# An adaLN block with a spectral filter and a gated bilinear MLP, forward and backward: the backward norms formed from two independent halves, the gate folded into a transform table, first activations of the tail loaded in the loop

## Chip, cores and metric

The kernel runs on one core of a Trainium2 chip. The metric is the device time of one execution in microseconds (us). The core's engines are named as in the profile: PE (TensorE matmul; PEld is its weight load), DVE (VectorE), ACT (ScalarE), POOL (GpSimd) and SP (SyncE, which here issues most of the DMA transfers). Each engine works through its own instructions in order and waits on semaphores.

## What is computed

The reference computes a block with two residual branches and the gradients of all its inputs (reference.py, cut):

```python
mod = (_silu(c) @ w_mod).reshape(c.shape[0], 6, 1, -1)
sa, ca, ga, sb, cb, gb = ...
h = _layernorm(x, axis=-1) * (1 + ca) + sa
x = x + ga * _A_ref(h, A_w_r, A_w_i)      # y = irfft2(rfft2(h) * (w_r + 1j * w_i))
h = _layernorm(x, axis=-1) * (1 + cb) + sb
x = x + gb * _B_ref(h, ...)               # ((h @ w_gate) * (h @ w_up)) @ w_down
...
_out, _vjp = jax.vjp(_f, A_x, A_w_r, A_w_i, B_w_gate, B_w_up, B_w_down, c, w_mod)
_grads = _vjp(grad_out)
```

The sequence has S = 2048 rows (16 tiles of 128), D = 576 channels, F = 4608 hidden channels; inputs and outputs are bf16. The gradient through a layer norm with normalised input n, reciprocal deviation r, and incoming gradient g (already times 1 + c) is r * (g - mean(g) - n * mean(g * n)). Here it is added to the gradient that comes along the residual path.

## The kernel before

**The whole.** The kernel first does the forward of the spectral branch with matrices in place of the FFT (about the first 210 us), then one loop over 36 blocks of 128 hidden channels, then a tail. The loop (`for fb in range(NFB)`) forms gate and up products (gup, L647), their gradients, the weight gradients of gate, up and down (u57p, L594) and the gradient of the MLP's input (u8p, L676), which DVE adds up over all blocks in SBUF (acc, L681). A block takes 28 us. For u8p the transposed weights of four blocks at a time lie in a tile wT, in a pool of two buffers (`wtp`); the last of them, for blocks 32 to 35, leaves the other buffer without further use. The gradient of the MLP's hidden product, ghh, is loaded per block on POOL's queue; the transposing DMAs of hh, gg and gu are on SP's.

**The tail** starts when tile t of acc is whole; its instructions are interleaved with the last block's by a scheduler that works with priorities (`HEAD_START`, `SPREAD`), so the order in the queues is not the order in the text. The PE instructions of the last blocks' u57p, and of out_0's matrix product (u3p, L1127), serve as fill between the steps of the tail. The tail has these stages:

- T1 (L852 to L921), 16 tiles in a pipeline of four steps. `t1_norm`: from acc(t) it forms ghr (ACT copy, L869), gn = acc * (1 + cb) with its row sum (DVE, L872), the row sum of gn * n2 (jk, L874), the two means as a pair ab (L876), then u = gn * r + ab0 (ACT, L878), v = n2 * ab1 + u (DVE, L880), gxr = v + goc (DVE, L881; goc is a tile of grad_out, and gxr is stored as gx1_d for T3) and gyr = gxr * ga (DVE, L883; ga_h is the gate as a row, copied to all partitions). `t1_turn`: five PE transposes of gyr (trp, L888), an ACT copy (gyT, L890), and the column sums and diagonals csA, csB, csC (L784, L791) for the modulation's gradients, which use ghr, gxr, n2 and y (tile yc). `t1_cols`: gyT times the row transform's table RD (zp, L908), copied by ACT (zt, L909). `t1_rows`: zt times the table G1 (vp, L915 and L916), copied into Vp.
- T2 (L963 to L1011), 19 chunks: the filter in the frequency domain, with transposes trv (L971) and try_ (L995), products xp and apt, and wn, the weights w_r and w_i (one load of all of it, L930 on).
- T3 (L1024 to L1069), 16 tiles in a pipeline of three steps: the inverse transform (upa, upb, yp) and `t3_norm`, the backward of the first norm, with the same chain as T1: gn (L1049), jk (L1051), abt (L1053), u (L1055, ACT), v (L1057), ob = v + gxc (L1059), stored as the gradient of x.
- the rest of u3p with its outputs, and the gradients of the modulation's weight (`section`, L812).

**Loads of the tail.** SP loads, for each pair of tiles of T1, n2c, goc and yc (288 KB each, L857), with the tables RD (730 KB) behind the first pair and G1 (1536 KB) behind the second (an explicit order, `behind(ld["order"])`). All three tiles have two buffers. The w_down weights for u3p are loaded in two tiles, wdA (15 blocks) and wdB (21 blocks), beside tiles hl of hh (L1102, L1113), issued after a T1 load (`after`) and as soon as their place in SBUF is free. SBUF space is given by pools, and a new tile waits for the last user of the addresses it takes.

Of the kernel before, what the change touches and what calls it, by code (L numbers as in the profile page):

```python
# [9 lines left out]
FP32 = mybir.dt.float32  # L10
# [9 lines left out]
NT = 16  # L20
# [64 lines left out]
def build(ctx, tc, A_x, A_w_r, A_w_i, B_w_gate, B_w_up, B_w_down, c_in, w_mod, grad_out,  # L85
# [36 lines left out]
    dsl_col = glob.tile([128, 5], FP32, name="dsl_col")  # L122
    ident = glob.tile([128, 128], BF, name="ident")
# [419 lines left out]
    with ExitStack() as ms:  # L543
# [8 lines left out]
        ga_h = c1a.tile([128, D], BF, name="ga_h")  # L552
# [4 lines left out]
        with ExitStack() as bs:  # L557
# [18 lines left out]
            nc.sync.dma_start(ga_h[:], modb_d[:, MGA, :])  # L576
# [42 lines left out]
            def wT_load(f0, after):  # L619
                nb = min(FBT, NFB - f0)  # L620
                wT = wtp.tile([128, 2, FBT, D], BF, name="wT")
# [67 lines left out]
            for fb in range(NFB):  # L689
# [7 lines left out]
                if fb == 0:  # L697
                    wTs[0] = wT_load(0, turns[-1:] * 5)
                ghh = ghp.tile([128, NT, 128], BF, name="ghh")
# [31 lines left out]
    with ExitStack() as ts:  # L731
# [108 lines left out]
        with ExitStack() as r1:  # L840
# [5 lines left out]
            rings = {k: c1b.tile([128, 3, DP], BF, name=k) for k in ("gyr", "ghr", "gxr")}  # L846
# [3 lines left out]
            ld, gyTs, zts = {"order": []}, {}, {}  # L850

            def t1_norm(t):  # L852
                if t % 2 == 0:
                    for k, src in (("n2c", n2_d), ("goc", go_v), ("yc", y_d)):
                        ld[k] = c1.tile([128, 2, D], BF, name=k)
                        with behind(ld["order"]):
                            ins = nc.sync.dma_start(ld[k][:], src[:, t:t + 2, :])  # L857
                        if t == 4:
                            ld["after"] = ins.ins
                    if t < 4:  # L860
                        ld["order"] = [ins.ins]
                        with behind(ld["order"]):
                            for k, tag in ((("RD", "tA"),), (("G1", "tB"), ("BD2", None), ("BDA", None)))[t // 2]:
                                T[k] = load_table(tl0, k, tag)
                        ld["order"] = [tab_ins[k]]
                    ld[t // 2] = (ld["n2c"], ld["yc"])
                n2 = ld["n2c"][:, t % 2, :]
                gh, gx, gy = (rings[k][:, t % 3, 0:D] for k in ("ghr", "gxr", "gyr"))
# [5 lines left out]
                nc.vector.scalar_tensor_tensor(out=jk[:], in0=gn[:], scalar=1.0, in1=n2, op0=MUL, op1=MUL, accum_out=s12[:, 1:2])  # L874
# [10 lines left out]
            def t1_turn(t):  # L885
                pt = ps_fp.tile([128, 5, 128], BF, name="trp", tag="fp")
                for m in range(5):
                    nc.tensor.transpose(pt[:, m, :], rings["gyr"][:, t % 3, wide(m)], ident[:])  # L888
# [338 lines left out]
```

## Time and profile before

Three executions took 1585.04, 1588.66 and 1589.61 us; the profile is of another execution of 1585.66 us.

| what | value |
|---|---|
| time, median of 3 runs | 1588.66 us |
| profiled execution, its time | 1585.66 us |
| profiled execution, its span | 1583.9 us |
| mean granted PE clock | 0.99 |
| PE busy | 1526.4 us, 96% of the span |
| DVE busy | 1043.3 us, 66% |
| ACT busy | 559.4 us, 35% |
| POOL busy | 172.3 us, 11% |
| DMA traffic | 280.33 MB, mean 177 GB/s |

How to read it: the profile shows one execution. "Busy" is the time in which an engine executes instructions; a line of a group gives the source line, the engine and operation, output and inputs by the program's names, partitions x elements, then busy time and mean ns of one, then the idle time ahead of such instructions and what ended it. A line of waits gives engine, operation and line, then what released it, the total in us, how often, and the longest. In a table by stretch, each engine's busy time is followed by its number of instructions in brackets; PEclk is the granted clock of PE as a share of the full one, and DMA share the busy share of the 16 DMA engines. Matmuls are pipelined, so the mean duration of one (286 ns for a 288-column one) is longer than the distance between two; 32 u57p in a row took 3.92 us.

### The profile page before, as it was taken

How to read it: one execution, taken by the hardware profiler on the slowest of the kernel's cores; microseconds unless marked ns; L12 is line 12 of the kernel's file. 1: busy time of each engine (PE TensorE's matmuls, PEld its weight loads, DVE VectorE, ACT ScalarE, POOL GpSimd, SP SyncE). 2: the span in 40 equal slices, each digit the busy share in tenths (PEclk: the TensorE clock that was granted, in tenths of full speed). 3: DMA queues.
4: the chain of work that ended last, by engine and by line, in shares of the span. 5: the costliest groups of instructions: out<-in, count | busy, mean ns of one | idle time of the engine just before them, and what ended most of it. 6: DMA issues, size and time to landing. Idle time of an engine off the chain costs nothing.

```text
span 1583.9 us, 29938 instructions
## 1 busy us (share of the span) xinstructions
PE 1526.4 (96%) x11300; PEld 1028.1 (65%) x11306; DVE 1043.3 (66%) x2626; ACT 559.4 (35%) x1120; POOL 172.3 (11%) x285
## 2 busy tenths in 40 slices
PE   6999999999999999999999999999999979799997
PEld 4665543566666666667666666766666666577775
DVE  6866663766666666666666666666666765678655
ACT  6667732322222222222222222222222356465022
POOL 0001221110010101001010100101000002000232
PEclk9999999999999999999999999999999999999999
DMA  9879997868685795877767786858976777547775
GB/s 323 268 197 235 289 261 211 172 133 158 123 177 114 159 153 118 168 132 155 141 148 136 143 163 122 173 116 144 139 141 137 193 207 200 212 144 214 278 228 156
DMA packets 485252, 280.33 MB, mean 177 GB/s; under 512 B 407634, under 2 KB 452435, under 8 KB 484211
## 3 DMA queue, kind: packets, MB, share of 16 engines
q1 hardware_dynamic: 459922, 185.50, 54.9%
q0 software_dynamic: 25184, 92.92, 19.7%
q8 instruction: 88, 1.44, 0.4%
q14 instruction: 58, 0.47, 0.1%
HBM read 108.48 MB, written 82.31 MB: 120 GB/s over the span
## 4 chain that ended last, share of the span: by engine, by line
PE 81%; DVE 6%; DMA 5%; issue 4%; ACT 3%; POOL 0%; SPq 0%; ACTq 0%; DVEq 0%; POOLq 0%
PE u57p L594 26%; PE u8p L676 18%; PE gup L647 16%; PE u4p L408 7%; PE u3p L1127 4%; PE gup L642 2%; DMA Xn<-xn_d 2%; DMA n2c<-n_d 2%; PE yp L186 1%; PE zp L908 1%; ACT u L1055 1%; PE zp L346 1%; DVE ln_st L151 1%; DMA xc<-in_A_x_dram 1%; DMA hh_sf<-hhT 1%
## 5 line engine op out<-in xcount | busy, mean ns | idle before, releaser
L681 DVE TENSOR_TENSOR acc<-acc,u8p 128x288 f32<-128x288 f32 x1088 | 489.2, 454 | 314.6 <-PE u8p L676 314.2
L676 PE MATMUL u8p<-wT,ggT 128*128 128x288 bf16 x1152 | 327.5, 286 | 1.7 <-DVE acc L681 1.7
L676 PE MATMUL u8p<-wT,guT 128*128 128x288 bf16 x1152 | 327.2, 286 | 0.0
L647 PE MATMUL gup<-h2T,wgu 128*128 128x512 bf16 x1152 | 294.9, 379 | 0.0
L597 ACT CAST so<-u57p 128x288 bf16<-128x288 f32 x216 | 86.0, 398 | 521.4 <-PE u57p L594 515.5
L594 PE MATMUL u57p<-gon,hh_sf 128*128 128x288 bf16 x1152 | 188.5, 286 | 0.5 <-DMA hh_sf<-hhT 0.5
L594 PE MATMUL u57p<-h2p,gg_sf 128*128 128x288 bf16 x1152 | 187.9, 286 | 0.0
L594 PE MATMUL u57p<-h2p,gu_sf 128*128 128x288 bf16 x1152 | 185.9, 286 | 0.0
L647 PEld LDWEIGHTS <-wgu 128*128 128x128 bf16 x1152 | 109.5, 98 | 98.8 <-issue 17.1
L676 PEld LDWEIGHTS <-ggT 128*128 128x128 bf16 x1152 | 112.6, 98 | 67.2 <-issue 14.0
L408 PE MATMUL u4p<-goT,wdT 128*128 128x512 bf16 x656 | 151.6, 380 | 0.6 <-DVE goT L380 0.5
L676 PEld LDWEIGHTS <-guT 128*128 128x128 bf16 x1152 | 112.7, 98 | 55.8 <-issue 2.2
L1127 PEld LDWEIGHTS <-hl 128*128 128x128 bf16 x1152 | 111.9, 99 | 32.9 <-issue 5.9
L594 PEld LDWEIGHTS <-hh_sf 128*128 128x128 bf16 x1152 | 112.7, 98 | 29.2 <-DMA hh_sf<-hhT 0.8
L594 PEld LDWEIGHTS <-gu_sf 128*128 128x128 bf16 x1152 | 112.5, 98 | 28.4
L594 PEld LDWEIGHTS <-gg_sf 128*128 128x128 bf16 x1152 | 112.5, 98 | 28.2
L649 ACT CAST gT<-gup 128x512 bf16<-128x512 f32 x144 | 84.3, 586 | 130.7 <-PE gup L647 130.7
L649 ACT CAST uT<-gup 128x512 bf16<-128x512 f32 x144 | 84.3, 585 | 73.5 <-PE gup L647 73.5
L408 PEld LDWEIGHTS <-wdT 128*128 128x128 bf16 x656 | 61.4, 98 | 73.1 <-issue 8.0
L1127 PE MATMUL u3p<-wdB,hl 128*128 128x288 bf16 x672 | 94.8, 290 | 5.3 <-DMA wdB<-in_B_w_down_dram 5.3
L660 POOL DMA_DIRECT2D hhT_d<-hhT x36 | 33.2, 921 | 504.4 <-DVE hhT L651 475.5
L141 ACT CAST ghh_st<-u4p 128x512 bf16<-128x512 f32 x88 | 51.2, 585 | 65.2 <-PE u4p L408 63.7
(357 smaller groups left out, 1701.7 us busy)
## 6 DMA issues: line engine op xcount, KB each, us to landing
ghhT_d<-ghh_st POOLq DMA_DIRECT2D x36, 512.0 KB, 4.4
ghh<-ghhT_d POOLq DMA_DIRECT2D x36, 512.0 KB, 7.3
hhT_d<-hhT POOLq DMA_DIRECT2D x36, 512.0 KB, 6.6
hl<-hhT_d SPq DMA_DIRECT2D x32, 576.0 KB, 7.2
out_dram<-woT SPq DMA_DIRECT2D x72, 128.0 KB, 2.0
wdn<-in_B_w_down_dram SPq DMA_DIRECT2D x18, 288.0 KB, 3.9
out_dram<-so SPq DMA_DIRECT2D x36, 144.0 KB, 2.6
wgu<-in_B_w_gate_dram SPq DMA_DIRECT2D x18, 256.0 KB, 3.4
```

The lines of the kernel that those rows point to most:

```text
L141: nc.scalar.copy(dst, src)
L151: nc.vector.bn_stats(out=st[:, t, h, :], in_=xt[:, t, h * 288:(h + 1) * 288])
L408: nc.tensor.matmul(pt[:], lhsT=wdTs[k][:, j, m, :], rhs=goT[:, 4 * sb4:4 * sb4 + 4, m, :], start=(m == 0 and n == 5), stop=(m == n - 1))
L594: mm = nc.tensor.matmul(pw[0][:, 0:288], lhsT=sf[:, t, :], rhs=rhs_n[:, t, h * 288:(h + 1) * 288], start=(t == 0), stop=(t == NT - 1))
L597: nc.scalar.copy(so[:, h * 288:(h + 1) * 288], pw[0][:, 0:288])
L642: nc.tensor.matmul(pts[-1][:], lhsT=wgu[r, 8, jw * 128:(jw + 1) * 128], rhs=h2T[r, 4 * sb4:4 * sb4 + 4, 4, :], start=True, stop=False)
L647: nc.tensor.matmul(pts[k][:], lhsT=wgu[:, 4 * wi_ + m, jw * 128:(jw + 1) * 128], rhs=h2T[:, ts_, m, :], start=False, stop=(m == 3))
L649: nc.scalar.copy((gT, uT)[wi_][:, ts_, :], pts[k][:])
L660: nc.gpsimd.dma_start(hhT_d[:, :, fb, :].rearrange("tp f x -> f tp x"), hhT[:].rearrange("f (tp ti) p -> f tp (ti p)", ti=2))
L676: nc.tensor.matmul(pu[:, 0:288], lhsT=l_, rhs=r_, start=(k == 0), stop=(k == len(mms) - 1))
L681: nc.vector.tensor_tensor(out=dst, in0=dst, in1=pu[:, 0:288], op=ADD)
L1127: mm = nc.tensor.matmul(p2[:, 0:288], lhsT=hls[fb // 9][:, fb % 9, ti * 128:(ti + 1) * 128], rhs=(wdA[:, fb] if fb < 15 else wdB[:, fb - 1 ...
```

## The change

Three things are done.

1. In both backward norms the result is formed from two halves. w = gn * r + (residual gradient) needs neither mean and is formed by DVE right behind the sums; u = n * ab1 + ab0 is formed by ACT from n instead of from gn; a last addition w + u gives gx (T1) or ob (T3). In T1 and in T3 this last part is a step of its own in the pipeline (`t1_gx`, `t3_out`), one turn later than the sums. The instruction v is gone.
2. The gate ga no longer multiplies the rows. gyr and its ring are gone, the transposes take gxr, and the rows of the table RD are multiplied by ga instead, once, by five ACT instructions on 128 x 584 elements in block NFB-2 of the loop. For this, ga is loaded as a column (two small DMAs, a POOL memset, a DVE copy), and the row ga_h is gone.
3. RD and the first two tiles of n2 are loaded by POOL in block NFB-3 of the loop, into a tile `early` in the pool of wT. n2 of tiles 2 to 7 is loaded in three pieces to one tile n2a at the head of the tail, in the place (tag tA) where RD was; n2c serves tiles 8 to 15 alone, and its first two loads are issued at t = 2 and 4. G1 is loaded at t = 0; goc has three buffers. The explicit order among these loads is gone.

The number of PE instructions is the same. In the built program, the loads of wdA stand behind opca_h on SP and wait for PE instructions of T1, and no u3p stands before T2's second apt.

```diff
--- before.py
+++ after.py
@@ -120,6 +120,8 @@
     rstd1g = glob.tile([128, NT], FP32, name="rstd1g")
     rstd2g = glob.tile([128, NT], FP32, name="rstd2g")
     dsl_col = glob.tile([128, 5], FP32, name="dsl_col")
+    ga_bf = glob.tile([128, 5], BF, name="ga_bf")
+    ga_col = glob.tile([128, 5], FP32, name="ga_col")
     ident = glob.tile([128, 128], BF, name="ident")
     make_identity(nc, ident[:])
     ones_f = glob.tile([128, 128], FP32, name="ones_f")
@@ -549,7 +551,7 @@
         c1acm = tc.tile_pool(name="c1a", bufs=1, side="right", reuse_waits="tile")
         c1a = c1acm.__enter__()
         opcb_h = c1a.tile([128, D], BF, name="opcb_h")
-        ga_h = c1a.tile([128, D], BF, name="ga_h")
+        ahead = {}
 
         def acc(t):
             return acc1[:, t, :] if t < 9 else acc2[:, t - 9, :]
@@ -573,7 +575,11 @@
             u8ps = bpool("u8ps", 3, PSUM)
             u57ps = bpool("u57ps", 2, PSUM)
             nc.sync.dma_start(opcb_h[:], modb_d[:, MCB, :])
-            nc.sync.dma_start(ga_h[:], modb_d[:, MGA, :])
+            nc.gpsimd.memset(ga_bf[:], 0.0)
+            with nc.allow_non_contiguous_dma(reason="tiny column load"):
+                nc.sync.dma_start(ga_bf[:, 0:4], modb_d[0, MGA, 0:512].rearrange("(m q) -> q m", q=128))
+                nc.sync.dma_start(ga_bf[0:64, 4:5], modb_d[0, MGA, 512:576].rearrange("(m q) -> q m", q=64))
+            nc.vector.tensor_copy(ga_col[:], ga_bf[:])
             pend = []
             NSO = 4
             so4 = sop.tile([128, NSO, DP], BF, name="so4")
@@ -618,7 +624,7 @@
 
             def wT_load(f0, after):
                 nb = min(FBT, NFB - f0)
-                wT = wtp.tile([128, 2, FBT, D], BF, name="wT")
+                wT = wtp.tile([128, 2, FBT, D], BF, name="wT", tag="wT")
                 for wi_, wsrc in enumerate((B_w_gate, B_w_up)):
                     for m in range(5):
                         K = KD[m]
@@ -696,6 +702,16 @@
                             eng.dma_start(wgu[64 * wi_:64 * wi_ + 64, 8, :], wsrc[512:576, fb * 128:(fb + FBW) * 128])
                 if fb == 0:
                     wTs[0] = wT_load(0, turns[-1:] * 5)
+                if fb == NFB - 3:
+                    early = wtp.tile([128, 2, FBT, D], BF, name="early", tag="wT")[:].rearrange("q i j d -> q (i j d)")
+                    RDg = early[:, 0:10 * FP].rearrange("q (m c f) -> q m c f", m=5, c=2)
+                    nc.gpsimd.dma_start(early[:, 0:10 * FP], tab_d["RD"][:, :])
+                    for t in range(2):
+                        ahead[t] = early[:, 10 * FP + t * D:10 * FP + t * D + D]
+                        nc.gpsimd.dma_start(ahead[t], n2_d[:, t, :])
+                if fb == NFB - 2:
+                    for m in range(5):
+                        nc.scalar.activation(out=RDg[:, m], in_=RDg[:, m], func=ACT.Copy, scale=ga_col[:, m:m + 1])
                 ghh = ghp.tile([128, NT, 128], BF, name="ghh")
                 with later(1, fb):
                     nc.gpsimd.dma_start(ghh[:].rearrange("f t p -> f (t p)"), ghhT_d[fb * 128:(fb + 1) * 128, :])
@@ -843,58 +859,75 @@
             csA = ps_cs.tile([128, 512], FP32, name="csA")
             csB = ps_cs.tile([128, 512], FP32, name="csB")
             csC = ps_cs.tile([128, 512], FP32, name="csC")
-            rings = {k: c1b.tile([128, 3, DP], BF, name=k) for k in ("gyr", "ghr", "gxr")}
+            rings = {k: c1b.tile([128, 3, DP], BF, name=k) for k in ("ghr", "gxr")}
             with tc.high_priority(HEAD_START):
                 for k in rings:
                     nc.vector.memset(rings[k][:, :, D:DP], 0.0)
-            ld, gyTs, zts = {"order": []}, {}, {}
+            ld, gyTs, zts = {}, {}, {}
+
+            def t1_loads(t):
+                if t == 0:
+                    n2a = tl0.tile([128, 6, D], BF, name="n2a", tag="tA")
+                    for k in range(3):
+                        ld["n2a"] = nc.sync.dma_start(n2a[:, 2 * k:2 * k + 2, :], n2_d[:, 2 + 2 * k:4 + 2 * k, :])
+                        for i in range(2):
+                            ahead[2 + 2 * k + i] = n2a[:, 2 * k + i, :]
+                        if k == 0:
+                            ld[0] = [c1.tile([128, 2, D], BF, name=n_, bufs=b_) for n_, b_ in (("goc", 3), ("yc", 2))]
+                            for tl_, src in zip(ld[0], (go_v, y_d)):
+                                nc.sync.dma_start(tl_[:], src[:, 0:2, :])
+                            T["G1"] = load_table(tl0, "G1", "tB")
+                    for k in ("BD2", "BDA"):
+                        T[k] = load_table(tl0, k)
+                if t % 2 == 0 and t:
+                    ld[t // 2] = [c1.tile([128, 2, D], BF, name=n_, bufs=b_) for n_, b_ in (("goc", 3), ("yc", 2))]
+                    for tl_, src in zip(ld[t // 2], (go_v, y_d)):
+                        ins = nc.sync.dma_start(tl_[:], src[:, t:t + 2, :])
+                    if t == 4:
+                        ld["after"] = ins.ins
+                if t in (2, 4, 12, 14):
+                    t_ = t + 6 if t < 8 else t
+                    n2c = c1.tile([128, 2, D], BF, name="n2c")
+                    nc.sync.dma_start(n2c[:], n2_d[:, t_:t_ + 2, :])
+                    for i in range(2):
+                        ahead[t_ + i] = n2c[:, i, :]
 
             def t1_norm(t):
-                if t % 2 == 0:
-                    for k, src in (("n2c", n2_d), ("goc", go_v), ("yc", y_d)):
-                        ld[k] = c1.tile([128, 2, D], BF, name=k)
-                        with behind(ld["order"]):
-                            ins = nc.sync.dma_start(ld[k][:], src[:, t:t + 2, :])
-                        if t == 4:
-                            ld["after"] = ins.ins
-                    if t < 4:
-                        ld["order"] = [ins.ins]
-                        with behind(ld["order"]):
-                            for k, tag in ((("RD", "tA"),), (("G1", "tB"), ("BD2", None), ("BDA", None)))[t // 2]:
-                                T[k] = load_table(tl0, k, tag)
-                        ld["order"] = [tab_ins[k]]
-                    ld[t // 2] = (ld["n2c"], ld["yc"])
-                n2 = ld["n2c"][:, t % 2, :]
-                gh, gx, gy = (rings[k][:, t % 3, 0:D] for k in ("ghr", "gxr", "gyr"))
+                t1_loads(t)
+                gh = rings["ghr"][:, t % 3, 0:D]
                 nc.scalar.copy(gh, acc(t))
                 s12 = c1.tile([128, 2], FP32, name="s12")
                 gn = c1.tile([128, D], BF, name="gn2")
                 nc.vector.scalar_tensor_tensor(out=gn[:], in0=acc(t), scalar=1.0, in1=opcb_h[:], op0=MUL, op1=MUL, accum_out=s12[:, 0:1])
                 jk = c1.tile([128, D], BF, name="jk2", bufs=1)
-                nc.vector.scalar_tensor_tensor(out=jk[:], in0=gn[:], scalar=1.0, in1=n2, op0=MUL, op1=MUL, accum_out=s12[:, 1:2])
+                nc.vector.scalar_tensor_tensor(out=jk[:], in0=gn[:], scalar=1.0, in1=ahead[t], op0=MUL, op1=MUL, accum_out=s12[:, 1:2])
                 ab = c1.tile([128, 2], FP32, name="ab2")
                 nc.vector.tensor_scalar(out=ab[:], in0=s12[:], scalar1=-1.0 / D, scalar2=rstd2g[:, t:t + 1], op0=MUL, op1=MUL)
+                w = c1.tile([128, D], BF, name="w2")
+                nc.vector.scalar_tensor_tensor(out=w[:], in0=gn[:], scalar=rstd2g[:, t:t + 1], in1=ld[t // 2][0][:, t % 2, :], op0=MUL, op1=ADD)
+                ld["ab", t], ld["w", t] = ab, w
+
+            def t1_gx(t):
+                gx = rings["gxr"][:, t % 3, 0:D]
                 u = c1.tile([128, D], BF, name="u2")
-                nc.scalar.activation(out=u[:], in_=gn[:], func=ACT.Identity, bias=ab[:, 0:1], scale=rstd2g[:, t:t + 1])
-                v = c1.tile([128, D], BF, name="v2", bufs=1)
-                nc.vector.scalar_tensor_tensor(out=v[:], in0=n2, scalar=ab[:, 1:2], in1=u[:], op0=MUL, op1=ADD)
-                nc.vector.tensor_tensor(out=gx, in0=v[:], in1=ld["goc"][:, t % 2, :], op=ADD)
+                ab = ld["ab", t]
+                nc.scalar.activation(out=u[:], in_=ahead[t], func=ACT.Identity, bias=ab[:, 0:1], scale=ab[:, 1:2])
+                nc.vector.tensor_tensor(out=gx, in0=ld["w", t][:], in1=u[:], op=ADD)
                 nc.gpsimd.dma_start(gx1_d[:, t, :], gx)
-                nc.vector.tensor_tensor(out=gy, in0=gx, in1=ga_h[:], op=MUL)
 
             def t1_turn(t):
                 pt = ps_fp.tile([128, 5, 128], BF, name="trp", tag="fp")
                 for m in range(5):
-                    nc.tensor.transpose(pt[:, m, :], rings["gyr"][:, t % 3, wide(m)], ident[:])
+                    nc.tensor.transpose(pt[:, m, :], rings["gxr"][:, t % 3, wide(m)], ident[:])
...
-                n2c, yc = ld[t // 2]
+                yc = ld[t // 2][1]
                 if t == 0:
                     add_zero(csA, csB, csC, first=True)
...
-                diag(csA, csB, 288, gh, n2c[:, t % 2, :])
+                diag(csA, csB, 288, gh, ahead[t])
                 diag(csC, csB, 352, gx, yc[:, t % 2, :])
                 if t == NT - 1:
                     add_zero(csA, csB, csC, first=False)
@@ -905,7 +938,7 @@
                     zp = ps_fp.tile([128, 512], FP32, name="zp", tag="fp")
                     for m in range(5):
                         with behind(fill[t - 1:t] if t else []):
-                            nc.tensor.matmul(zp[:, :FP], lhsT=gyTs[t][:, m, :], rhs=T["RD"][:, m, cc, :], start=(m == 0), stop=(m == 4))
+                            nc.tensor.matmul(zp[:, :FP], lhsT=gyTs[t][:, m, :], rhs=RDg[:, m, cc, :], start=(m == 0), stop=(m == 4))
                     nc.scalar.copy(zt[:, cc, :], zp[:, :FP])
 
             def t1_rows(t):
@@ -916,7 +949,7 @@
...
 
-            steps = [t1_norm, t1_turn, t1_cols, t1_rows]
+            steps = [t1_norm, t1_gx, t1_turn, t1_cols, t1_rows]
             for k in range(NT + len(steps) - 1):
                 with tc.high_priority(HEAD_START + SPREAD * k):
                     for s_ in reversed(range(len(steps))):
@@ -1051,13 +1084,9 @@
             nc.vector.scalar_tensor_tensor(out=jk[:], in0=gn[:], scalar=1.0, in1=n1, op0=MUL, op1=MUL, accum_out=s12[:, 1:2])
             ab = c3.tile([128, 2], FP32, name="abt")
             nc.vector.tensor_scalar(out=ab[:], in0=s12[:], scalar1=-1.0 / D, scalar2=rstd1g[:, sa:sa + 1], op0=MUL, op1=MUL)
-            u = c3.tile([128, D], BF, name="u1")
-            nc.scalar.activation(out=u[:], in_=gn[:], func=ACT.Identity, bias=ab[:, 0:1], scale=rstd1g[:, sa:sa + 1])
-            v = c3.tile([128, D], BF, name="v1", bufs=1)
-            nc.vector.scalar_tensor_tensor(out=v[:], in0=n1, scalar=ab[:, 1:2], in1=u[:], op0=MUL, op1=ADD)
-            ob = c3.tile([128, D], BF, name="ob1")
-            ld3["last"] = nc.vector.tensor_tensor(out=ob[:], in0=v[:], in1=ld3["gxc"][:, sa % 2, :], op=ADD).ins
-            nc.sync.dma_start(o1_v[:, sa, :], ob[:])
+            w = c3.tile([128, D], BF, name="w1")
+            nc.vector.scalar_tensor_tensor(out=w[:], in0=gn[:], scalar=rstd1g[:, sa:sa + 1], in1=ld3["gxc"][:, sa % 2, :], op0=MUL, op1=ADD)
+            ld3[sa] = (n1, ab, w)
             if sa == 0:
                 add_zero(csD, csE, first=True)
             for h in range(2):
@@ -1066,7 +1095,15 @@
             if sa == NT - 1:
                 add_zero(csD, csE, first=False)
 
-        pipeline(NT, [t3_rows, t3_cols, t3_norm])
+        def t3_out(sa):
+            n1, ab, w = ld3[sa]
+            u = c3.tile([128, D], BF, name="u1")
+            nc.scalar.activation(out=u[:], in_=n1, func=ACT.Identity, bias=ab[:, 0:1], scale=ab[:, 1:2])
+            ob = c3.tile([128, D], BF, name="ob1")
+            ld3["last"] = nc.vector.tensor_tensor(out=ob[:], in0=w[:], in1=u[:], op=ADD).ins
+            nc.sync.dma_start(o1_v[:, sa, :], ob[:])
+
+        pipeline(NT, [t3_rows, t3_cols, t3_norm, t3_out])
         dca = diag_rows(tl, csD, csE, 288, "dca")
         dsa = tl.tile([128, 288], FP32, name="dsa")
         nc.vector.tensor_copy(dsa[:], csE[:, 0:288])
```

## The prediction

> **What bounds the kernel now.** I read first the page's busy shares and the chain that ended last (PE holds 81% of it, the loop's matmuls by far the most), then busy time by stretch of the tail, where the change acts.
>
> ```profile
> core 0: us, PE busy (x) PEld busy (x) DVE busy (x) ACT busy (x) POOL busy (x), PEclk, DMA share, GB/s
> 1236.50:1259.50 23.00, 21.30 (x171) 16.40 (x169) 20.75 (x56) 5.58 (x9) 0.90 (x1) 1.00 1.04 284
> 1259.50:1280.00 20.50, 19.72 (x200) 15.37 (x199) 15.13 (x42) 14.24 (x29) 3.26 (x6) 1.00 0.47 134
> 1280.00:1300.00 20.00, 12.21 (x105) 9.13 (x104) 13.23 (x35) 8.58 (x17) 2.69 (x5) 0.85 0.86 261
> 1300.00:1342.20 42.20, 39.45 (x352) 29.07 (x351) 21.05 (x52) 26.42 (x55) 6.71 (x13) 0.99 0.65 175
> 1342.20:1370.00 27.80, 19.22 (x178) 14.05 (x180) 16.26 (x46) 10.99 (x22) 4.50 (x11) 0.88 0.85 319
> 1370.00:1404.50 34.50, 33.00 (x345) 24.07 (x344) 28.52 (x88) 21.03 (x46) 3.78 (x7) 1.00 0.42 138
> 1404.50:1458.00 53.50, 50.98 (x455) 38.57 (x455) 43.61 (x115) 35.80 (x85) 0.55 (x1) 1.00 0.57 164
> 1458.00:1500.00 42.00, 42.00 (x345) 33.55 (x343) 27.46 (x60) 4.00 (x9) 9.66 (x18) 1.00 0.82 296
> ```
>
> Rows 1 to 4 are the first backward norm with its transform (T1, to 1342.2), 5 and 6 the filter stage (T2), 7 the second norm (T3), 8 pure u3p. The second column is length, the third PE's busy time. PE idles 1.70 + 0.78 + 7.79 + 2.75 = 13.0 us in T1, 8.6 in the head of T2, 1.5 in its rest, 2.5 in T3, nothing in row 8. So PE bounds the kernel, and a change here gains only what it takes from these 25.6 us and from the low clock behind the longest waits.
>
> ```profile
> 1292.00:1296.00 4.00, 0.52 (x5) 0.51 (x5) 0.46 (x1) 0.00 (x0) 0.00 (x0) 0.74 1.29 325
> 1296.00:1300.00 4.00, 4.00 (x25) 2.91 (x24) 3.17 (x10) 1.40 (x3) 0.54 (x1) 0.50 0.38 83
> 1352.00:1356.00 4.00, 0.00 (x0) 0.00 (x0) 0.20 (x1) 0.00 (x0) 0.00 (x0) 0.92 1.01 368
> 1356.00:1360.00 4.00, 3.61 (x25) 2.90 (x25) 0.93 (x3) 1.10 (x3) 0.00 (x0) 0.50 1.08 362
> ```
>
> Two waits are each followed by 4 to 6 us at clock 0.50: half of 4, about 2 us, lost at 1296, and some 2.9 at 1356. Which waits:
>
> ```profile
> PE csA L791 <- DMA n2c<-n_d: 8.1, 4, 6.7
> PE u3p L1127 <- DMA wdB<-in_B_w_down_dram: 5.3, 1, 5.3
> ```
>
> The first (PE, waits from 1228 to 1410; total, times, longest) is T1's; the second is the head of T2, where the change does not name anything but moves the transfers ahead of it. The DMA issues of 1225 to 1345 (KB each, median us to landing) say why n2c is late:
>
> ```profile
> wn<-wn_d POOLq DMA_DIRECT2D x1, 2336.0 KB, 12.3
> n2c<-n_d SPq DMA_DIRECT2D x8, 288.0 KB, 3.2
> T_G<-tab_G SPq DMA_DIRECT2D x1, 1536.0 KB, 11.9
> T_RD<-tab_RD SPq DMA_DIRECT2D x1, 730.0 KB, 8.9
> ```
>
> In the chain of 1200 to 1345, n2c's pieces are 9.14 us (from 1241.13, beside RD) and 9.50 us (from 1285.95, beside wn) instead of 3.2.
>
> **Part 1, the gate leaves the row and enters the table.** Sixteen gyr products go (DVE, L883), and each tile's dependent chain changes:
>
> ```profile
> L878 ACT ACTIVATE u<-gn,ab,rstd2g 128x576 bf16<-128x576 bf16 x16 | 13.7, 867 | 12.9 <-DVE ab L876 12.9
> L880 DVE SCALAR_TENSOR_TENSOR v<-n2c,ab,u 128x576 bf16<-128x576 bf16 x16 | 13.0, 815 | 0.3
> L883 DVE TENSOR_TENSOR gyr<-gxr,ga_h 128x576 bf16<-128x576 bf16 x16 | 7.2, 455 | 7.0 <-PE trp L888 7.0
> ```
>
> After ab it was u 867, v 815, gxr 451, gyr 455: 2588 ns. Now w (form of v, 815) does not depend on ab, so u 867 and gx 451 remain: 1318 ns, 1.27 us shorter. DVE loses 16 x 455 ns = 7.3 us in T1, where it is busy 70.2 of 105.7, so this alone is worth nothing; the shorter chain counts where PE waits for gxr or gyr, 0.5 us in the waits (trp on gyr). The price: five scalings of the table in the loop. The trace has no 128x584 Copy with a per-partition scale; the nearest rows are 128x576 ones, 757 to 867 ns, so 5 x 0.87 = 4.35 us of ACT at fb 34. ACT is busy 7.1 of 28 us in an iteration, so PE loses 0 by cover, and at most 1.7 us if two of them stand ahead of uT without slack: I take 0.5. The gate's column (two tiny loads, a DVE copy placed near 94 to 98 us, in the forward) waits for the modulation's store; gbT's column loads took 2.5 to 4.1 us to land and DVE is idle about 0.7 to 1 us there: 0 to 1, I take 0.5. A further DVE wait is bounded by that same idle.
>
> **Part 2, loads.** RD (730 KB) and n2 tiles 0 and 1 go into the loop, into the second wT buffer, on POOL's queue behind ghh of fb 34, whose use is a full iteration away; the DMA share there is 0.57 to 0.73, and 730 + 288 KB at 370 GB/s are 2.8 us of it: nothing. In T1, n2 for tiles 2 to 7 comes in one six-tile buffer and tiles 8 to 11 are fetched early, so the 8.1 us wait for n2c goes, and its 2 us of low clock: T1 without any wait is 105.7 - 13.0 - 2 = 90.7. It does not get there. In the built order of the changed program, (a) SP issues n2a's first piece, G1 and two n2c (288 + 1536 + 576 KB) ahead of goc 0, which w(0) needs: 2400 KB at 280 GB/s (first row) are 8.6 us, so from 1239 to about 1249 with issue time; (b) DVE holds the norms of tiles 0 to 6 ahead of the last 17 acc additions (L681), so gx(0) ends near 1256, while PE has run out of what stands ahead of its transposition by 1252.6 (its matmuls counted at 0.123 us each, from the chain's 32 u57p in 3.92): about 4 us of wait; behind the transposition stand the remaining u8p halves. (c) yc keeps two buffers, and its loads now wait for csC of two pairs before: one wait of 2 us beside wn's 2336 KB. Together about 6.5 idle and up to 2 cold: 90.7 + 8.5 = 99.2. T1 -6.5. From below: waits (a) to (c) hidden, -15; from above: goc takes T_G's whole 11.9 us instead of 8.6 and yc an n2c's 9.5 instead of 3.2, together 9.6 more, +3.
>
> The Trainium skill, "DMA: Bandwidth & Descriptors", section Queues, rings and completion order, says that each DMA engine consumes the descriptors of one issuer's ring in ring order, which speaks against putting G1 ahead of goc. The trace agrees (n2c behind RD took 9.14 us); by the rule alone goc 0 lands behind all 2400 KB, as I have it; were the transfers served side by side, goc 0 would come in some 4 us and T1 gain 4 us more.
>
> **Part 3, the first u3p weights.** The early buffer lies where wdA goes. Before, wdA's halves (1152 + 1008 KB) were issued at 1328.6 and 1333.2, 14 and 9 us ahead of T1's end; now both wait for the last zp, 2 us before it, behind opca_h. So 2160 KB, 5.8 us at the 372 GB/s of that stretch, come ahead of hl and wdB. The built order has no u3p before T2's second apt (before: 15 at its head): u3p in T2 223 to 193, in T3 65 to 42, after T3 864 to 917. These 53 cost 53 x 0.125 = 6.6 us (895 in 111.7 us) wherever they stand; moved behind, they are a loss only if T2 and T3 do not shrink by as much. T2's first chunks have no fill for about 7.5 us, and 2 cold; before, 8.6 idle (5.3 of it for wdB, whose use now comes about 19 us into T2) and 2.9 cold. I take -1.5; ends -5 (no cold stretch, wdB in time) and +8 (rival C).
>
> The Trainium skill, "TensorE: Matmul & The Clock Gate", section Part 1: The HAM clock gate, says that an idle window of about 3.4 us halves the clock until a busy window of that length has passed. The trace agrees (6.7 and 5.3 us of wait, then 4 to 6 us at 0.50); by it, waits of 4 us before tile 0 and 7.5 in T2's head cost 1.7 each, which the sums above bound by their own rows at 2.
>
> **Part 4, T3.** The split leaves DVE's count: gn 755, jk 755, abt 225, w for v 817, ob 453 = 3.0 us a tile, against 53.5 / 16 = 3.3 now; PE's share falls by 23 x 0.125 = 2.9 to 48.1, or 3.0. DVE's 6.3 us of waiting on u go. Both engines are then even: T3 shrinks by about the 2.9 moved out: 0, from -2 (its 2.5 idle gone) to +3 (it keeps its length).
>
> **Sum.** -6.5 + 0.5 + 0.5 - 1.5 + 0 = -7.0. Against the profiled execution, 1585.66 us (span 1583.9), this is 1578.7; that execution lies 3.0 under the median of the runs shown, 1588.66, so on the median's scale 1581.7, say 1582. The same steps with every wait in its place give 1573 to 1587, the likeliest case's own range.
>
> **Rivals.**
> A, larger gain (0.10): no wait in (a) to (c), T1 -15, T2 as forecast: 1588.66 - 15.5 = 1573. For it: DVE's idle 35.5 us in T1; against: the 24 DVE operations of tiles 0 to 6 ahead of the additions.
> B, the wait only moves (0.22): PE waits for gx(0) and yc as it did for n2c, T1 -1 to -2, the rest +1: 1588. This is the case in which not n2 held T1 but the 2336 KB of wn, whose neighbours are late whatever they are.
> C, slower (0.26): the transfers that the change packs ahead of goc 0 and behind T1's last zp move at 195 GB/s, the mean of 1225 to 1345, instead of 280 and 372. Then goc 0 comes 2400 KB / 195 - 8.6 = 3.7 us later. In T2, PE is in order, and its first u3p, about 8.4 us in, needs wdA and hl: 2160 + 1152 KB take 17 us from 2 us before T2, so PE stops for 6.6 us with T2's chunks behind it, and 2.9 are cold. 13.2 in all, on -7.0: +6.2, 1595. It outweighs the gain below about 250 GB/s (1.0 + 2.9 + 2.9 there). For it: the same stretch already held the wait for wdB, at a DMA share of 0.85 to 1.29; against: 319 GB/s in its row now.
>
> **How the numbers follow.** The forecast has 0.42. Changes under 0.3%, 4.8 us, cannot be told from none here. Faster: A 0.10, the forecast's 0.36, 0.03 of B: 0.49. Same: B 0.17, 0.05 of the forecast, 0.03 of C: 0.25. Slower: C 0.23, 0.02 of B, 0.01 of the forecast: 0.26. Range 1571 to 1597: A's centre and most of C inside.
>
> **What would show it.** Right: no gyr rows, w at about 815 ns, no PE wait for n2; a PE wait of 3 to 5 us before the first transposition of gxr near 1252; wdA issued after the last zp; T1 ending near 1336; no u3p in T2's first 8 us; T3 at 3.0 to 3.2 us a tile. Wrong: T1's end later than 1340, a wait of u3p for hl or wdA over 3 us, PE idle in the loop at fb 34, or T3 as long as before.

## The result, and the profile after

The changed kernel took 1601.91 us in the median of 4 runs (1598.29 to 1606.14), the kernel before 1589.13 us (4 runs). The ratio is 1.0094 with a 95% interval of 1.0071 to 1.0118: about 15 us slower by the ratio, 12.8 us between the two medians, and the interval lies wholly above 1. The forecast was 1582, with a range to 1597.

The profiled execution of the changed kernel took 1603.45 us (span 1601.7), 17.8 us of span more than that of before. To see where, I read the same marks on PE in both traces: the start of the first gup (end of the forward), of the last gup (end of the loop), of the last zp (end of T1), of the last apt (end of T2), of the last yp (end of T3) and of the last gcp (end of PE's work). The differences are the lengths of the stages, in us:

| profile | forward | loop | T1 | T2 | T3 | rest |
|---|---|---|---|---|---|---|
| before | 273.7 | 962.4 | 104.7 | 63.5 | 49.4 | 126.4 |
| changed | 282.3 | 962.4 | 110.9 | 62.7 | 46.2 | 133.1 |
| difference | +8.6 | 0.0 | +6.2 | -0.8 | -3.2 | +6.7 |

T1, which was to shrink by 6.5, grew by 6.2. T2 and T3 shrank by 4.0 and the rest grew by 6.7, mostly because 51 u3p that stood in T2 and T3 now stand behind them (193 instead of 223 in T2, 40 instead of 61 in T3 by these marks). And the forward, where next to nothing was changed, took 8.6 us longer. The experiments below show that the kernel before varies there by as much from one execution to the next.

Busy time by stretch of the changed kernel (columns as before: stretch, length, then PE, PEld, DVE, ACT, POOL with instruction counts, clock, DMA share, GB/s); the first four rows are T1, then the head and the rest of T2, and T3:

```profile
1244.90:1264.00 19.10, 16.58 (x133) 12.70 (x130) 16.02 (x44) 5.77 (x10) 1.46 (x2) 1.00 0.93 310
1264.00:1282.00 18.00, 17.22 (x128) 12.48 (x129) 15.03 (x39) 6.90 (x14) 1.62 (x3) 0.91 0.81 136
1282.00:1300.00 18.00, 15.38 (x173) 11.72 (x172) 13.99 (x36) 12.85 (x24) 2.69 (x5) 1.00 0.52 161
1300.00:1357.20 57.20, 45.24 (x391) 33.55 (x394) 21.71 (x53) 30.07 (x63) 10.03 (x21) 0.91 0.50 135
1357.20:1384.00 26.80, 17.16 (x165) 13.49 (x166) 14.80 (x43) 11.14 (x21) 2.46 (x5) 0.75 1.04 374
1384.00:1418.50 34.50, 30.94 (x326) 22.39 (x323) 26.74 (x82) 20.17 (x44) 3.77 (x7) 1.00 0.48 161
1418.50:1467.00 48.50, 46.26 (x421) 35.65 (x421) 42.51 (x111) 35.98 (x83) 0.55 (x1) 1.00 0.49 132
```

PE's idle time in T1 is 2.5 + 0.8 + 2.6 + 12.0 = 17.9 us, against 13.0 before, and most of it now lies in the fourth row. The finer stretches show it as one hole and the low clock behind it:

```profile
1306.00:1310.00 4.00, 0.00 (x0) 0.00 (x0) 0.00 (x0) 0.47 (x2) 0.00 (x0) 0.92 0.87 68
1310.00:1314.00 4.00, 0.00 (x0) 0.00 (x0) 0.00 (x0) 0.00 (x0) 0.00 (x0) 0.50 1.00 390
1314.00:1318.00 4.00, 2.21 (x13) 1.55 (x13) 2.23 (x8) 0.93 (x2) 0.00 (x0) 0.50 0.53 181
```

PE's waits from 1228 to 1430 name its cause and the other new waits:

```profile
PE csA L807 <- DMA n2c<-n_d: 10.2, 2, 9.9
PE u3p L1164 <- DMA hl<-hhT_d: 4.7, 1, 4.7
PE trp L921 <- DVE gxr L915: 3.2, 1, 3.2
PE csC L807 <- DMA yc<-y_d: 2.3, 2, 1.7
```

So the wait for n2 did not go: it is 10.2 us instead of 8.1. Most of it belongs to another pair of tiles, 12 and 13. SP's queue shows how it came (start, duration, line, transfer):

```profile
1298.58 1.26 SPq L611 DMA_TRANSPOSE woT<-so  x1
1299.95 0.52 SPq L885 DMA_DIRECT2D yc<-y_d  x1
1300.57 0.68 SPq L885 DMA_DIRECT2D goc<-in_grad_out_dram  x1
1311.06 0.39 SPq L612 DMA_DIRECT2D out_dram<-woT  x1
1311.50 0.51 SPq L613 DMA_DIRECT2D out_dram<-woT  x1
1312.11 0.53 SPq L891 DMA_DIRECT2D n2c<-n_d  x1
```

n2 of tiles 12 and 13 is issued behind the store of woT, and the store waits on SP until woT's transposing DMA has landed, 12.5 us after its issue. POOL had issued wn's 2336 KB at 1295.15, and they took 12.7 us: the transpose and everything else in that stretch stood beside them. The chain of waits has the three long transfers of the tail as pieces (start, length):

```profile
1247.25 10.68 DMA goc<-in_grad_out_dram
1298.58 12.46 DMA woT<-so
...
1357.04 14.26 DMA hl<-hhT_d
```

The first is goc 0 behind G1, the third hl at the head of T2. Beside hl, two queues were then busy: wdA was loaded on SP's, and T3's table GB on POOL's, issued at 1357.16. Among the issues of 1240 to 1365 (KB, us to landing) they are:

```profile
T_GB<-tab_GB POOLq DMA_DIRECT2D x1, 1536.0 KB, 10.4
wdA<-in_B_w_down_dram SPq DMA_DIRECT2D x1, 1152.0 KB, 6.2
wdA<-in_B_w_down_dram SPq DMA_DIRECT2D x1, 1008.0 KB, 13.3
```

Between hl's issue at 1357.04 and its landing at 1371.30 the DMA engines moved 5.28 MB (370 GB/s), 3.55 of it on the queue that carries SP's loads and 1.70 on POOL's. In place of before's v and gyr the groups show 16 w of 816 ns and no gyr; T3's DVE no longer waits 6.3 us for u but 1.9.

### The profile page after: what moved, and what is told of

Its sections match the earlier page's. It is cut to its first block, busy times and chain, and to the rows that moved or that the text cites. A ratio compares the mean times of both kernels' runs of the same rounds, so it can differ in the third digit from the quotient of the medians.

```text
span 1601.7 us, 29954 instructions
## 1 busy us (share of the span) xinstructions
PE 1528.2 (95%) x11300; PEld 1028.7 (64%) x11306; DVE 1036.8 (65%) x2610; ACT 562.9 (35%) x1125; POOL 174.6 (11%) x289
## 4 chain that ended last, share of the span: by engine, by line
PE 80%; DVE 8%; DMA 7%; ACT 3%; issue 2%; SPq 0%; POOL 0%; DVEq 0%; ACTq 0%; POOLq 0%
PE u57p L600 26%; PE u8p L682 17%; PE gup L653 16%; PE u4p L410 7%; PE u3p L1164 4%; PE gup L648 2%; DMA xc<-in_A_x_dram 2%; DMA Xn<-xn_d 1%; PE zp L941 1%; DVE ln_st L153 1%; DMA hl<-hhT_d 1%; DMA woT<-so 1%; PE yp L188 1%; PE zp L348 1%; DMA goc<-in_grad_out_dram 1%
## 5 line engine op out<-in xcount | busy, mean ns | idle before, releaser
L410 PEld LDWEIGHTS <-wdT 128*128 128x128 bf16 x656 | 61.3, 98 | 77.5 <-issue 12.7
L1164 PE MATMUL u3p<-wdB,hl 128*128 128x288 bf16 x672 | 91.5, 286 | 0.0
```

Of the source, the lines that this page charges most:

```text
L410: nc.tensor.matmul(pt[:], lhsT=wdTs[k][:, j, m, :], rhs=goT[:, 4 * sb4:4 * sb4 + 4, m, :], start=(m == 0 and n == 5), stop=(m == n - 1))
L1164: mm = nc.tensor.matmul(p2[:, 0:288], lhsT=hls[fb // 9][:, fb % 9, ti * 128:(ti + 1) * 128], rhs=(wdA[:, fb] if fb < 15 else wdB[:, fb - 1 ...
```

## The experiments

All stage lengths below are read from the profile of each run, by the marks above. The times have several runs each of the experiment and of before on the same chip; "ratio" is to before.

**1. The forward.** The changed kernel loads the gate as a column near 94 us. This run adds only that to the kernel before:

```diff
+            nc.gpsimd.memset(ga_bf[:], 0.0)
+                nc.sync.dma_start(ga_bf[:, 0:4], modb_d[0, MGA, 0:512]...)
+                nc.sync.dma_start(ga_bf[0:64, 4:5], modb_d[0, MGA, 512:576]...)
+            nc.vector.tensor_copy(ga_col[:], ga_bf[:])
```

> The kernel before with nothing added but the gate's column (memset, two tiny loads on SP, one DVE copy); PE's and ACT's order are the same. In the changed kernel's profile the loop starts 8.6 us later (first gup at 282.3 instead of 273.7 us) with the same order of the forward. Theory: the two column loads, issued near 94 us into a stretch whose DMA share is about 1, shift the loads and transposes behind them, and that delay is theirs: first gup near 282, the whole 8 us slower (ratio about 1.005). Rival: it belongs to that one execution, or to something in the loop or the tail: first gup within 1.5 us of 273.7, ratio within 0.001 of 1.

Measured: ratio 1.0004 (0.9980 to 1.0028), with the first gup at 282.8 us in its profile. The profile said yes and the times said no. So a second profile of the kernel before was taken:

> The kernel before once more, for a second profile. First gup was at 273.7 and 276.4 us in two profiles without the early column loads, at 282.3, 282.8 and 277.8 in three with them, but the times of the kernel with the column alone were the same as before's (1.0004). Theory (the forward varies from execution to execution, whatever the column does): the first gup is off 273.7 by 2 us or more. Rival (the column delays it): within 2 us of 273.7.

Measured: the first gup at 283.7 us, 10 us later than in the first profile of the same kernel; every stage behind it was the same to within 0.9 us (loop 962.3, T1 103.8, T2 63.6, T3 49.4, rest 126.0). So the forward of an unchanged kernel differed by 10 us between two executions; its time varies as widely, from 1579.93 to 1598.17 us in 25 runs on one chip. Over all profiles, six without the early column have it at 273.7 to 283.7 (mean 277.8), eight with it at 277.8 to 284.2 (mean 280.8). The 8.6 us of the profiled pair therefore lie within such variation; whether some 3 us belong to the column stays open.

The third run on this moved the column's load into block 30 of the loop:

> The changed kernel with the gate's column loaded in the loop (block 30) instead of in the forward; all else in its order. Theory (column loads delay the forward): first gup back at 274, total near 1593, 8.6 us under the changed kernel, ratio to before about 1.004. Rival: first gup stays near 282, ratio about 1.009.

Measured: 1619.31 us, ratio 1.0178 (1.0124 to 1.0233). The forward was 275.6, but the loop took 985.6 instead of 962.4, so the total tells nothing about the column. What it tells is this:

```profile
DVE ga_col L707 <- DMA ga_bf<-modb_d: 19.3, 1, 19.3
```

In DVE's waits, its one tiny copy stood 19.3 us ahead of everything behind it, since the load was issued only when SP's queue came to it; the additions of acc stopped, and PE waited 16.0 us for them. I had placed load and copy at one place of the loop and forgot the queue between them.

**2. T3 alone.** The kernel before with the split and the fourth step in T3 only.

```diff
-            u = ...gn * rstd1g + ab0;  v = n1 * ab1 + u;  ob = v + gxc
+            w = ...gn * rstd1g + gxc
+        def t3_out(sa):
+            u = ...n1 * ab1 + ab0;  ob = w + u
```

> The kernel before with only T3's norm formed from two halves, with its fourth step. Theory: T3 gets shorter by what its fill of u3p loses, no more: from the last apt to the last yp 46 us instead of 49.4, the stretch behind it longer by about the same, ratio within 0.0015 of 1. Rival 1: the shorter chain is worth its own 1 to 3 us, ratio 0.998 to 0.999. Rival 2: T3 loses more fill than it gains, ratio 1.002.

Measured: ratio 0.9994 (0.9969 to 1.0019); T3 46.3 instead of 49.4, the rest 133.6 instead of 126.4. The built order has 42 u3p in T3 instead of 61, and 19 x 0.125 = 2.4 us of the longer rest are theirs; another 2.9 are a wait of csF for DVE's pr there. The remaining 1.9 us stay open. In the profile T3 gets shorter by 3.1, and nothing of it is left. The interval of the time holds the theory and rival 1 and ends just short of rival 2's 1.002; it does not decide among them.

**3. What holds n2.** Was it SP's queue, or wn? First n2 of tiles 12 to 15 was taken off SP:

```diff
-                    nc.sync.dma_start(n2c[:], n2_d[:, t_:t_ + 2, :])
+                    (nc.scalar if t >= 12 else nc.sync).dma_start(n2c[:], n2_d[:, t_:t_ + 2, :])
```

> The changed kernel with the loads of n2 for tiles 12 to 15 on ACT's queue instead of SP's. In the changed kernel n2 of tile 12 was issued at 1312.1, behind a store on SP that waited from about 1301 to 1311 for the transposing DMA of woT (issued 1298.6, beside wn's 2336 KB), and PE waited 9.9 us for it and then ran at clock 0.50. Theory (head of SP's queue): the wait falls to 3 us or less, T1 from last gup to last zp falls from 110.9 to 101 to 104 us, total 7 to 10 us under the changed kernel. Rival (wn's transfer itself): n2 is issued earlier but lands beside wn, the wait stays 6 us or more, T1 107 or more.

Measured: ratio 1.0060 (1.0031 to 1.0090), T1 108.6. My theory fell: the wait, and n2's issue on ACT's queue (start, duration), are

```profile
PE csA L807 <- DMA n2c<-n_d: 9.7, 2, 9.4
```
```profile
1298.98 0.35 ACTq L891 DMA_DIRECT2D n2c<-n_d  x1
```

Issued at 1299.0 on a queue that carried no other load, it released PE and DVE only at 1310.9, 11.9 us later. (The 10.2 us that the next expectation gives for it belong to two n2 loads at T1's head, issued at 1243.7 and 1244.1 beside G1.) Loads of yc and goc that SP issued at 1295.8 and 1296.6, also beside wn, took 13.5 and 15.5 us. The queue made n2 late in the one kernel, and the transfer itself in the other; what both have is wn. So wn was held back, in the changed kernel and in before, by a one-column copy of a T1 result into wn, for which the load must wait:

```diff
+        with tc.high_priority(HEAD_START + SPREAD * 14):
+            nc.vector.tensor_copy(wn[:, 0, 0, 0:1], Vv[:, 0, 7, 1, 0:1])
-        nc.gpsimd.dma_start(wn[:]..., wn_d)
+            nc.gpsimd.dma_start(wn[:]..., wn_d)
```

> The changed kernel with the load of wn (2336 KB) held back in T1: a one-column copy of a T1 result (tile 7) into wn precedes it, so it stands behind the store of gx 11 instead of gx 6 on POOL's queue; PE's order is the same. With n2 of tile 12 issued on ACT's queue it still landed 10.2 us after its issue, so SP's queue is not the cause. Theory (wn's transfer delays what stands beside it, wherever T1 then is): no wait for n2 over 2 us, T1 from last gup to last zp 99 to 101 us instead of 110.9, total 9 to 11 us under the changed kernel, ratio to before about 1.002. Rival 1: the transposing load of woT (12.5 us) is the slow one by itself: the wait for n2 stays over 5 us. Rival 2: wn, now late, is missing at the head of T2: T1 gains 10, T2 loses 5 or more.

> The kernel before with the same hold on wn's load (behind the store of gx 12). Theory: its 6.7 us wait for n2 and the 2 us of low clock go too, T1 from last gup to last zp falls from 104.7 to 96 to 98 us, ratio 0.994 to 0.996; then the T1 of the changed kernel without wn's collision (99 to 101) is no shorter than that of before without it. Rival: T1 of before stays over 102, because RD and G1 at its head or the longer chain hold it.

Measured: the changed kernel 1.0025 (1.0000 to 1.0050), T1 100.5; before 0.9966 (0.9949 to 0.9982), T1 97.4. Waits of the changed kernel so held, then of before so held:

```profile
PE csA L807 <- DMA n2c<-n_d: 1.4, 2, 1.1
```
```profile
PE csA L791 <- DMA n2c<-n_d: 3.6, 3, 2.5
```

In the changed kernel woT's transpose then landed in 4.0 us, not 12.5, which speaks against rival 1. So wn's load is what made n2 late in both kernels, and T2 did not miss it (62.7 and 63.7 us). Also, without wn in the way the T1 of the changed kernel is still 3.1 us longer than that of before. Something else in it costs.

**4. The head of T1.** goc 0 ahead of G1 and of the two early n2 loads on SP:

```diff
-                            for tl_, src in zip(ld[0], (go_v, y_d)): nc.sync.dma_start(...)
-                            T["G1"] = load_table(tl0, "G1", "tB")
+                            first = [nc.sync.dma_start(...).ins for tl_, src in ...]
+                            with behind(first[0:1]):
+                                T["G1"] = load_table(tl0, "G1", "tB")
```

> The changed kernel with only the order of SP's first loads in T1 changed: grad_out of the first tiles goes ahead of G1 and of two n2 loads, G1 behind it. In the changed kernel goc 0 was issued at 1247.3 and landed at 1257.9 (w of tile 0 waited for it 2.6 us on DVE), and PE waited 3.2 us for gxr 0. Theory (G1 ahead of goc costs the head of T1): that 3.2 us wait falls under 1.5 us and T1 from last gup to last zp falls by 2 to 4 us from 109 to 111. Rival (DVE's order, with the last additions of acc behind the first norms, sets the head): the wait stays over 2.5 us, T1 within 1 us, or G1, now late, is waited for by vp.

Measured: the wait of trp for gxr 0 falls from 3.2 to 0.5 us, and w's for goc is gone; T1 104.9, some 5 us less than in the three profiles with the changed kernel's own T1 order (110.9, 110.4 and 108.6). The time, 1.0077 (1.0046 to 1.0108), can't be told from the changed kernel's. In its 5 us are 2.7 for the wait itself and 2.1 by which the wait for n2 became shorter (7.8 instead of 9.9). DVE's order has a part in this wait, too: in the built program of both kernels gx of tile 1 stands on DVE ahead of gx of tile 0. In the changed kernel the two ended at 1261.2 and 1264.6; PE had run out of other work at 1261.5 and transposed tile 0 at 1264.7. Whether the wait would go with tile 0 first was not tried.

**5. T1's split alone.** The kernel before with w and u in T1, but with gyr, its loads and its tables as they were.

```diff
-                u = ...gn * rstd2g + ab0;  v = n2 * ab1 + u;  gx = v + goc
+                w = ...gn * rstd2g + goc;  u = ...n2 * ab1 + ab0;  gx = w + u
```

> The kernel before with only T1's norm formed from two halves: gyr and its gate product stay, loads and tables stay. Theory: T1 of before is held by n2, G1 and wn's transfers, not by the dependent chain, so from last gup to last zp it stays at 103 to 105 us, ratio within 0.002 of 1. Rival: the chain shorter by 0.8 us (one DVE operation off it) shortens T1 by 2 us or more.

Measured: ratio 1.0029 (1.0003 to 1.0056), T1 107.1, with 11.8 us of waits for n2 instead of 8.1. The shorter chain is worth nothing here; it is even a little slower, since the median time of n2 to landing was 4.3 us instead of 3.2. Why these loads fell so was not tried.

**6. The head of T2.** The two pools of w_down exchanged, so that wdB, not wdA, takes the early tile's place:

```diff
-        oAp = pool("oAp", 1)
-        oBp = pool("oBp", 1)
+        oBp = pool("oBp", 1)
+        oAp = pool("oAp", 1)
```

> The changed kernel with the two pools of w_down's tiles in the other order, so that wdA no longer lies where the early tile lies, and wdB does. In the built order wdA is then issued two transposes ahead of T1's end, and 13 u3p stand at the head of T2 again. Theory (the early tile's place held wdA back and cost T2 its fill): the 4.7 us wait for hl goes, u3p at T2's head; from the last zp to the last apt 61 to 64 us with some 30 more u3p in it, the stretch behind T3 3 us shorter: total 3 to 5 us under the changed kernel. Rival: wdB, now late, waits instead, total within 1.5 us of the changed kernel.

Measured: ratio 1.0054 (1.0033 to 1.0074). From the last zp to the end of PE's work it is 238.3 us, against 242.0 in the changed kernel and 239.3 in before; T2 is 63.0 with 222 u3p in it again. The place of wdA thus cost 3.7 us by the two profiles; the intervals of the two times touch and do not show it alone. Its two waits in T2's head, in place of the 4.7 for hl:

```profile
PE u3p L1164 <- DMA wdB<-in_B_w_down_dram: 2.1, 1, 2.1
...
PE u3p L1164 <- DMA hl<-hhT_d: 1.5, 1, 1.5
```

**7. All three taken back.** The changed kernel with goc first, wn held back and the pools exchanged:

> The changed kernel with three things taken back or moved: grad_out ahead of G1, wn held back as in after_wn, and wdA's and wdB's places exchanged as in swap. Theory (the parts add): T1 from last gup to last zp 97 to 99 us (after_wn 100.5, goc_first 2 to 3 less), behind it 3.5 us less than the changed kernel, the loop 0 to 3 us over before: ratio to before 0.994 to 0.998, about as before_wn (0.9966). Rival: the collisions only move again, T1 over 101, ratio 1.000 or more.

Measured: ratio 0.9986 (0.9957 to 1.0015), over the expected range, though the interval reaches into it. T1 is 95.5, the stages behind it 237.8; both are shorter than before's. But the loop took 965.1 us, as in after_wn, where it did not in the changed kernel's profile. ACT's and PE's waits in combo's loop:

```profile
ACT early L714 <- DMA early<-tab_RD: 3.6, 1, 3.6
```
```profile
PE u57p L600 <- ACT uT L655: 1.9, 1, 1.9
```

The table is loaded only some 4 us ahead of its scaling, and where it lands late, ACT holds uT behind it. The load took 5.0 us to land in the changed kernel's profile, 6.0 in swap, 6.8 in n2_act and 7.6 here; ACT's wait for it was 1.0, 2.0, 2.8 and 3.6 us, and the loop 962.4, 963.4, 964.4 and 965.1. So the scalings were put behind the last cast of the block after:

```diff
-                if fb == NFB - 2:
+                if fb == NFB - 1:
                     for m in range(5):
+                        with tc.issue_after(ahead["act"]):
-                        nc.scalar.activation(out=RDg[:, m], ...)
+                            nc.scalar.activation(out=RDg[:, m], ...)
```

> As combo, but the five scalings of the table by the gate stand on ACT behind the last cast of block 34 instead of between a gT and a uT of the block before. In combo's trace ACT waited 3.6 us for the table's load there, uT stood behind it, PE waited 1.9 us for uT, and the loop took 965.1 us instead of 962.4. Theory (a load issued a few us before its use, ahead of casts that PE needs): loop back to 962.4 to 962.6, total 2 to 3 us under combo, ratio to before 0.995 to 0.998. Rival (the loop's extra time is the load's bandwidth): the loop stays over 964.

Measured: loop 962.3, T1 95.8, the rest behind 238.2; 1581.61 us in the median of 12 runs against 1592.10 for before, ratio 0.9958 (0.9937 to 0.9979). The wait for the table is gone from ACT's waits. But in this execution the table landed in 5.0 us, as in the changed kernel's profile, whose loop took 962.4 without the new placement; and the intervals of combo and combo_late overlap. So what the placement saves is argued from the four waits above, not shown by this run.

combo_late is faster than both kernels. It has all three parts of the change, with four placements altered. Before with nothing but wn held back stands at 0.9966 (0.9949 to 0.9982); the two can't be told apart. The three parts so placed, but with wn where it was, were not run.

## Why the prediction was wrong, step by step

- **T1, "so the 8.1 us wait for n2c goes": the step that failed.** I gave n2's tiles 8 to 11 their early loads and did not follow tiles 12 to 15, whose two buffers come free only when 8 to 11 are done with. I also left wn as a neighbour of yc alone, "one wait of 2 us". In fact wn stands on POOL's queue behind stores of gx1, behind that of tile 6 (before: tile 5), and was issued 50.4 us into T1 instead of 45.9; its 12.7 us met woT's transposing DMA and, held up behind that on SP, the load for tiles 12 and 13, which PE then needed. The wait was 10.2 us in all instead of none, and the clock fell to 0.50. Rival B had this mechanism ("not n2 held T1 but the 2336 KB of wn"), with a price too small: it gave T1 back its old length, where the wait came out longer than the one it replaced.
- **The floor, 90.7 for T1 without any wait**: borne out. PE was busy 90.47 of combo's 95.5 us.
- **(a) and (b), goc behind G1, about 4 us of PE's wait**: right in place and size (3.2, at the transposition of tile 0; goc 0 landed 13.2 us into T1, and the forecast's 1249 is 12.9 us into it). The 2 us for yc in (c) came, too: csC waited 2.3 us for it. The rule from the Trainium skill, "DMA: Bandwidth & Descriptors", section Queues, rings and completion order, that a ring's descriptors are consumed in order, agrees with the trace: goc 0 took 10.7 us behind G1, and w no longer waited for it ahead of G1. This order also more than accounts for the 3.1 us by which the changed T1 is longer once wn is away: with goc first (and the pools exchanged), combo's T1 is 95.5, against 97.4 in before_wn and 100.5 in after_wn.
- **T2, -1.5.** The mechanism was right (wdA blocked, no fill), the size was off: from T1's end on the changed kernel took 2.8 us more, not 1.5 less. I had 7.5 us of idle head with u3p in time; the first u3p came 15.8 us into T2 instead of 8.4, with a 4.7 us wait for hl. Rival C named this wait, for a slower DMA than there was: the head moved 374 GB/s, not 195, and hl still landed 14.3 us after its issue. So it was not the rate. The sum has 2160 KB of wdA and 1152 of hl, from 2 us before T2 on. In the trace wdA was issued 0.3 us into T2, and beside it POOL moved T_GB's 1536 KB, which no term of mine has. Where wdA was issued ahead of T1's end and hl ahead of T_GB, in before, swap and combo, the first hl landed in 4.5, 4.4 and 4.7 us. How much of the 14.3 us is T_GB's and how much wdA's, no run separates. swap puts the place of wdA at 3.7 us.
- **T3, 0**: right. It shrank by 3.2 and the u3p moved out of T2 and T3 took 51 x 0.125 = 6.4 of the 6.7 us by which the rest grew.
- **The loop, +0.5 for ACT's scalings, and "nothing" for the loads**: a wrong reason. The profiles show no loss from the 3.8 us of scaling themselves (loop 962.4 in both kernels); what went with a longer loop, by 0 to 2.7 us, was the wait ahead of them for a load issued some 4 us before.
- **The column, +0.5**: can't be told; ga_only bounds it between -3 and +4 us.

Added up from profiles with like orders: T1 6.1 longer (110.9, 110.4 and 108.6, against 104.7, 103.8, 103.4 and 103.5), what stands behind it 4.3 longer (mean of changed, n2_act, goc_first, after_wn and ga_late, 243.2, against 238.9 of before, before_again, ga_only and before_wn), and the loop by 0 to 2.7. That is 10 to 13 us, at the lower end of the 11 to 19 that the interval allows; what the forward has of the remainder stays open.

## What to carry to other kernels

When a load is taken away from a stretch, look for the largest transfer in that stretch first: if another 2 MB stands there, the wait moves to whatever is loaded next to it, and holding the large one back gained 0.34% alone here, where the change as it was made lost 0.94%. Follow each queue through all the tiles, not only the ones that are prefetched, and ask of every reused buffer which later load must now wait for it. A load and its use at one place of the text need distance in the queues: a few microseconds of lead turned harmless work on idle engines into a stall of the engine that bounds the kernel.

## What was not expected of the hardware

- Two executions of the same program had the forward stage end at 273.7 and 283.7 us, with all later stages equal to within 0.9 us. From 150 to 240 us, in that stage, the DMA share was 1.06 and 1.05 in the two. A single pair of profiles can show a difference of 9 us there that no change made.
- A transposing DMA took 12.5 us beside a 2336 KB load, and 4.0 us with that load held back. 288 KB loads of n2, 3.2 us at the median, took 9.5 beside it on SP's queue (before) and 11.9 on ACT's (n2_act).
- After the hole of about 9.9 us PE ran at clock 0.50 until past 1318 us, and at the head of T2 the stretch from 1357.2 to 1384 had a mean of 0.75: each of these waits cost a second time.
